# Attention scores and probabilities as pairs of 64-row products, k without masks, PSUM banks divided three, two and three

## The chip, the cores and the metric

One Trainium2 chip, of which the program uses one core. TensorE (PE in the traces, its weight loads PEld) multiplies and transposes; VectorE (DVE), ScalarE (ACT) and GpSimd (POOL) work on tensors; SyncE (SP) issues nearly all DMA. PSUM, where TensorE writes, has eight banks of 128 partitions x 512 float32. The metric is the device time of one execution in microseconds (us), lower is better. The kernel before takes 1148.17 us in the median of three runs (1147.83 to 1148.45).

## The reference

Three layers, one after the other, all in float32:

```
k_p, v_p = mean of k, v over groups of 8 positions            # (4, 8, 72, 64)
attn     = softmax(q @ k_p.T / 8)                             # (4, 8, 576, 72)
x        = (attn @ v_p), heads side by side                   # (2304, 512)

p   = domain_probs / domain_probs.sum(-1)
x   = sum over 4 experts e of  p[:, e] * (relu(x @ w1[e]) @ w2[e])     # 512 -> 1024 -> 512

out = (((x @ g_w1) * (x @ g_w2)) @ g_w3) @ g_wout             # 512 -> 1024 -> 1024 -> 512
```

Four batches, eight heads of 64, 576 positions each; so 2304 tokens of 512 numbers. Pooling leaves 72 keys for each head.

## The kernel before

**Stages.** The tokens are cut into 18 tiles of 128 and six blocks of 384 (three tiles). Attention is done tile by tile. A lead does tiles 0 to 2 alone; the other tiles are slipped into the first expert, whose units (one block, one of eight slices of 128 hidden columns) follow each other in `run_first`: `begin_unit` makes 12 products for a hidden slice, `end_unit`, two units later, 9 products into three accumulators of the block (L1212). Between the steps stands a gap, and `hooks[n]` lists the attention pieces of gap n. The lists are written out in the code (L690 to L726); no planner decides. After the first expert come the other three experts, a stage on w3 and w_out, and the gated layer; none of these is touched, except that their ring of eight PSUM banks (`bank_r`) runs over the banks in another division.

**Attention of one batch.** `load_k` brings the pooled rows in five chunks, four of 128 rows (a row is head and key) and a tail of 64; `pool_k` adds eight positions into one row of 64. Then it makes a row of 128 with the 64 numbers twice, times a mask `mk`: the left copy stays where the head is even, the right where it is odd, zeros elsewhere. Batch 0 does this on VectorE (sum) and GpSimd (mask); batch 1 on GpSimd, with the mask on ScalarE for four chunks (`mask_k`); batches 2 and 3 as batch 0. `make_kT` turns each chunk with a TensorE transpose; column j of kT then has its 64 numbers in partitions 0 to 63 for an even head, 64 to 127 for an odd one.

**Attention of one tile.** q of a tile is laid out as four pairs of heads, the even head's 64 numbers in the lower partitions, the odd one's in the upper. `scores`: one product for each pair, 128 rows deep, 144 columns (72 keys of each head; the zeros of the mask keep the heads apart). Two pairs fill one bank, four heads in a half. Tiles 4 and 13 straddle two batches and do it once for each half of the tokens, on 64 of the 128 output partitions. `exps`: maximum, subtraction and exponential, half by half. `sums`, `normalise`: division by the sum. `attn_T`: eight transposes (one per head, 128 tokens x 72 to 72 x 128), four to a bank, two pieces called one after the other, each followed by a ScalarE eviction into `at_t`. `attend`: for each pair of heads two products of 72 rows into the two halves of the output partitions (x_ps), then a split of the result into a high and a low part.

**PSUM banks.** Eight banks: q0 to q3 by name, and a pool p of four that are handed out in turn. During the first expert the hidden slices use q0 and q1, the attention q2 and q3 in turn (`spare`, cut to two at L1169, in the lead all eight), the three accumulators of a block three of the four in p, one further each time. The second half of batch 1's kT takes one of p.

Of the kernel before, what the change touches and what calls it, by code (L numbers as in the profile page):

```python
# [17 lines left out]
def fused_kernel(  # L18
# [16 lines left out]
    nc = tc.nc  # L35
# [295 lines left out]
    with tc.manual_schedule():  # L331
# [5 lines left out]
            ("at", (H // 2) * BLK * 4, 2), ("e", H * NK * 4, 3), ("kT", NCH * P * 4, 2), ("vp", H * D * 4, 2), ("qT", NP * P * 4, 1),  # L337
            ("kp", D * 4, 4), ("mx", H * 4, 2), ("sm", H * 4, 3), ("hm", NCH * H * 4, 1), ("mk", NCH * 2 * 4, 1),
# [14 lines left out]
        hm = ap.tile([P, NCH, H], F32, tag="hm", name="hm", bufs=1)  # L353
        nc.gpsimd.memset(hm, 1.0)
        nc.gpsimd.affine_select(out=hm, in_=hm, pattern=[[P, NCH], [-NK, H]], compare_op=ALU.is_ge,
                                fill=0.0, base=0, channel_multiplier=1)
        nc.gpsimd.affine_select(out=hm, in_=hm, pattern=[[-P, NCH], [NK, H]], compare_op=ALU.is_ge,
                                fill=0.0, base=NK - 1, channel_multiplier=-1)
        mk = ap.tile([P, NCH, 2], F32, tag="mk", name="mk", bufs=1)
        nc.vector.tensor_reduce(mk, hm.rearrange("p c (a b) -> p c b a", b=2), axis=AX.X, op=ALU.add)  # L360

# [49 lines left out]
        def pool_k(b, c, eng=nc.vector):  # L411
            if c == 0:
                kb_t[b] = ap.tile([P, NCH, 2, D], F32, tag="kb", name="kb", bufs=1)
# [22 lines left out]
        kp_t = {}  # L436

        def mask_k(c):
            for a in range(2):
                nc.scalar.activation(kb_t[1][:, c, a], kp_t[c], AF.Copy, scale=mk[:, c, a:a + 1])  # L440

        def make_kT(b, g0, g1):
            if g0 == 0:
                kT_t[b] = ap.tile([P, NCH * P], F32, tag="kT", name="kT")
            pt = bank_p("kT_ps") if b == 1 and g0 else bank("kT_ps")
# [5 lines left out]
            nc.scalar.activation(kT_t[b][:, g0 * P:g1 * P], pt[:, :(g1 - g0) * P], AF.Copy, scale=LOGIT)  # L451
# [71 lines left out]
        def scores(t):  # L523
            qT = qT_t.pop(t)
            sc_t[t] = []
            for half in range(2):
                sc = bank("sc")
                for hp in range(2 * half, 2 * half + 2):
                    for off, n, b, s in segments(t * P, P):
                        nc.tensor.matmul(sc[off:off + n, (hp % 2) * W:(hp % 2 + 1) * W],  # L530
                                         qT[:, hp, off:off + n], kT_t[b][:, hp * W:(hp + 1) * W],
                                         start=True, stop=True)
                sc_t[t].append(sc)
# [34 lines left out]
        def attn_T(t, half):  # L568
            i, o = divmod(t, TPB)
            if o == 0:  # L570
                at_t[i, half] = ap.tile([P, G, BLK], F32, tag="at", name="at")
# [66 lines left out]
        def do_turn(t):  # L638
            return [(None, lambda half=half: attn_T(t, half)) for half in range(2)]
# [22 lines left out]
        def weight(eng):  # L662
            return [(None, lambda: stream.split(eng))]
# [20 lines left out]
        def lower():  # L684
# [10 lines left out]
                + do_qT(3) + k1[:4] + do_attend(0) + [(None, lambda: rest_of_q.pop(0)())] + weight(VE) + [(None, lambda: mask_k(0)), (None, lambda: rest_of_q.pop(0)())])  # L695
# [4 lines left out]
        hooks[0] = [(None, lambda c=c: mask_k(c)) for c in range(1, NCH - 2)]  # L700
# [12 lines left out]
        hooks[at[TPB + 2] + 3][:0] = [hooks[at[TPB + 2] + 2].pop()]  # L713
# [455 lines left out]
        spare[:] = spare[:2]  # L1169
# [392 lines left out]
```

## Time and profile before

| what | value |
|---|---|
| runs | 1147.83, 1148.17, 1148.45 us |
| the profiled execution | 1147.9 us, its span 1146.1 us |
| TensorE busy | 1139.6 us (99%) |
| VectorE, ScalarE, GpSimd busy | 793.1, 376.0, 416.8 us |
| granted TensorE clock | 1.00 throughout |
| chain that ended last | 96% TensorE |
| score products (L530) | 160, from 10.4 to 160.6 us |
| transposes of probabilities (L575) | 144, from 16.6 to 174.8 us |
| x_ps products (L587) | 128, from 20.7 to 179.4 us |

The span runs from the first to the last instruction; the execution's own time has 1.8 us more around it. TensorE's instructions overlap: the duration in a row includes the way through the array, so the cost of one is read from its start to the start of the next. A row of the timeline that covers several instructions begins with the first and ends with the last; the time from its start to the start of the next row is what the group took. A float32 product appears as two matmuls in the trace, a transpose as one.

### The profile page before, as it was taken

The numbers are of one execution on the slowest core, as the hardware profiler recorded it, in microseconds if no ns is written. First come the engines' busy times: TensorE is split into PE (matmuls) and PEld (weight loads), VectorE is DVE, ScalarE is ACT, GpSimd is POOL, SyncE is SP. The second block draws the span as 40 slices with busy tenths as digits, with TensorE's granted clock in tenths as the row PEclk, the third lists the DMA queues.
The fourth block names the chain that finished last, engine by engine and source line by source line (L and its number), as shares of the span: only waits on it lengthen the run. The fifth ranks groups of instructions, "written<-read, shape, count | busy, mean of one in ns | idle before, by whom it ended". The sixth has DMA issues, their size and how long they took to land.

```text
span 1146.1 us, 17173 instructions
## 1 busy us (share of the span) xinstructions
PE 1139.6 (99%) x5985; PEld 1032.0 (90%) x5985; DVE 793.1 (69%) x1456; ACT 376.0 (33%) x672; POOL 416.8 (36%) x381
## 2 busy tenths in 40 slices
PE   8999999999999999999999999999999999999998
PEld 7898888999899898989898989989889999999997
DVE  7776544867768598658679578877786675774554
ACT  5643432345313053504134421314353313230110
POOL 6765213334525166524336642515001111331211
PEclk9999999999999999999999999999999999999999
DMA  9965515445966726495854578785476165947341
GB/s 229 229 148 123 186 62 197 166 152 183 322 220 196 235 80 181 142 316 167 263 152 123 182 237 192 238 208 146 145 195 230 43 261 209 333 152 288 112 166 56
DMA packets 211555, 213.85 MB, mean 187 GB/s; under 512 B 86596, under 2 KB 166796, under 8 KB 211468
## 3 DMA queue, kind: packets, MB, share of 16 engines
q1 hardware_dynamic: 211180, 212.23, 59.6%
q8 instruction: 47, 0.77, 0.3%
q10 hardware_dynamic: 288, 0.52, 0.1%
q14 instruction: 40, 0.33, 0.1%
HBM read 140.87 MB, written 71.83 MB: 186 GB/s over the span
## 4 chain that ended last, share of the span: by engine, by line
PE 96%; DVE 1%; POOL 1%; ACT 1%; DMA 0%; issue 0%; POOLq 0%
PE g L176 18%; PE g L174 18%; PE g L175 18%; PE s L174 13%; PE s L175 13%; PE s L176 13%; PE sc L530 1%; PE x_ps L587 1%; PE at_ps L575 1%; ACT ap L549 0%; DVE ap L419 0%; DMA stxh<-in_k_dram 0%; DVE ap L543 0%; POOL stxh L422 0%; POOL stxh L421 0%
## 5 line engine op out<-in xcount | busy, mean ns | idle before, releaser
L1014 DVE TENSOR_TENSOR plain<-s,plain 128x384 f32<-128x384 f32 x300 | 158.4, 554 | 83.5 <-PE s L176 35.4
L180 POOL TENSOR_TENSOR round<-x5l,round 128x768 fp32r<-128x768 f32 x60 | 112.2, 1870 | 271.5 <-ACT round L179 254.6
L176 PE MATMUL s<-xo,wl 128*128 128x384 f32 x624 | 208.6, 334 | 0.0
L174 PE MATMUL s<-xo,wh 128*128 128x384 f32 x624 | 208.6, 334 | 0.0
L175 PE MATMUL s<-xo,wh 128*128 128x384 f32 x624 | 208.5, 334 | 0.0
L174 PE MATMUL g<-w2l,round 128*128 128x512 f32 x522 | 204.8, 392 | 0.0
L176 PE MATMUL g<-w2h,round 128*128 128x512 f32 x522 | 203.8, 390 | 0.0
L175 PE MATMUL g<-w2h,round 128*128 128x512 f32 x522 | 203.5, 390 | 0.0
L174 PEld LDWEIGHTS s<-xo,wh 128*128 128x128 f32 x624 | 117.1, 188 | 0.5
L175 PEld LDWEIGHTS s<-xo,wh 128*128 128x128 f32 x624 | 117.1, 188 | 0.5
L176 PEld LDWEIGHTS s<-xo,wl 128*128 128x128 f32 x624 | 117.1, 188 | 0.0
L176 PEld LDWEIGHTS g<-w2h,round 128*128 128x128 f32 x522 | 97.9, 188 | 20.7
L174 PEld LDWEIGHTS g<-w2l,round 128*128 128x128 f32 x522 | 98.0, 188 | 20.0 <-issue 0.8
L175 PEld LDWEIGHTS g<-w2h,round 128*128 128x128 f32 x522 | 98.0, 188 | 19.4
L292 POOL TENSOR_TENSOR x5l<-x5l,x5h 128x256 uint32<-128x256 uint32 x80 | 60.6, 757 | 136.6 <-DVE x5h L291 128.3
L1018 ACT ACTIVATE plain<-s 128x384 f32<-128x384 f32 x60 | 29.2, 487 | 231.4 <-PE s L176 195.5
L179 ACT ACTIVATE round<-x5l 128x768 fp32r<-128x768 f32 x60 | 50.9, 848 | 147.7 <-DVE x5l L1422 146.6
L180 POOL TENSOR_TENSOR round<-plain,round 128x768 fp32r<-128x768 f32 (+1 forms) x29 | 52.5, 1812 | 117.7 <-ACT round L179 101.7
L286 DVE TENSOR_SCALAR x5l<-x5h 128x256 uint32<-128x256 uint32 x80 | 52.9, 662 | 50.3 <-DMA gate<-x5l 28.9
L1014 DVE TENSOR_TENSOR x5l<-s,plain 128x384 f32<-128x384 f32 x120 | 65.6, 556 | 24.8 <-PE s L176 18.3
L1260 ACT ACTIVATE plain<-plain 128x768 f32<-128x768 f32 x36 | 30.5, 848 | 111.3 <-DVE plain L1014 111.3
L174 PE MATMUL g<-xl,round 128*128 128x384 f32 x192 | 66.1, 344 | 0.0
(257 smaller groups left out, 2211.8 us busy)
## 6 DMA issues: line engine op xcount, KB each, us to landing
xo<-keptx SPq DMA_DIRECT2D x42, 768.0 KB
raw<-in_moe_w_dram SPq DMA_DIRECT2D x54, 256.0 KB
keptx<-xo SPq DMA_DIRECT2D x12, 768.0 KB
x5h<-in_moe_w_dram SPq DMA_DIRECT2D x128, 64.0 KB
x5h<-in_moe_w_dram SPq DMA_DIRECT2D x32, 256.0 KB
ob<-acc SPq DMA_DIRECT2D x24, 256.0 KB
kept<-xo SPq DMA_DIRECT2D x8, 768.0 KB
xo<-kept SPq DMA_DIRECT2D x8, 768.0 KB
```

The source lines that it names most:

```text
L174: nc.tensor.matmul(ps, lh, rl, start=first, stop=False)
L175: nc.tensor.matmul(ps, lh, rh, start=False, stop=False)
L176: nc.tensor.matmul(ps, ll, rh, start=False, stop=last)
L179: nc.scalar.activation(hi, src, AF.Copy)
L180: (lo_eng or nc.vector).tensor_tensor(lo, src, hi.bitcast(F32), op=ALU.subtract)
L286: nc.vector.tensor_scalar(au, h, 0x7FFFFFFF, None, op0=ALU.bitwise_and)
L292: nc.gpsimd.tensor_tensor(au, au, l, op=ALU.add)
L530: nc.tensor.matmul(sc[off:off + n, (hp % 2) * W:(hp % 2 + 1) * W], qT[:, hp, off:off + n], kT_t[b][:, hp * W:(hp + 1) * W], start=True, st ...
L575: nc.tensor.transpose(pt[:NK, g * P:(g + 1) * P], e[:, half * G + g, :], ident)
L1014: nc.vector.tensor_tensor(to, one, two, op=ALU.add)
L1018: nc.scalar.activation(x, product(j, A11, B11), AF.Copy)
L1260: nc.scalar.activation(r, r, AF.Relu)
```

## The change

- **k.** `pool_k` sums in three additions (256, 128, 64 columns), the last of which writes the row of 64 twice, with no mask. `mk`, `hm`, `kp`, `mask_k` and GpSimd's mask products are gone. The tail of 64 rows is transposed as 64 rows, and its columns alone are copied.
- **Scores.** For each pair of heads two products of 64 rows and 72 columns, the even head on partitions 0 to 63 into one bank, the odd head on 64 to 127 into another. A bank holds the four even or the four odd heads of all pairs, so the order of heads in `e` becomes even heads, then odd.
- **Probabilities.** Each of the eight transposes becomes two, of tokens 0 to 63 and 64 to 127, in two banks that alternate; one piece instead of two; the evictions write eight heads of 64 tokens each. `at_t` is one tile for a block.
- **Banks.** q0 to q4 and a pool p of three. The attention has q2, q3, q4 in turn during the first expert, the accumulators always the same three.

TensorE's rows at the end of the lead before (qT_ps turns q, sc are scores, vp_ps sums v, at_ps turns probabilities, x_ps is attention times v):

```order
L530 MATMUL sc<-ap_72,plain 128x144 x4
L509 MATMUL qT_ps<-ident,stxh 128x128 x4
L530 MATMUL sc<-ap_72,plain 128x144 x8
L469 MATMUL vp_ps<-stxl,ident 72x192 x8
L575 MATMUL at_ps<-ident,ap_72 72x128 x8
L469 MATMUL vp_ps<-stxl,ident 72x64 x8
L575 MATMUL at_ps<-ident,ap_72 72x128 x16
L587 MATMUL x_ps<-ap_72 64x384 x8
```

The same place now:

```order
L505 MATMUL sc<-ap_72,plain 128x72 x8
L485 MATMUL qT_ps<-ident,stxh 128x128 x4
L505 MATMUL sc<-ap_72,plain 128x72 x16
L445 MATMUL vp_ps<-stxl,ident 72x192 x8
L552 MATMUL at_ps<-ident,ap_72 72x64 x16
L445 MATMUL vp_ps<-stxl,ident 72x64 x8
L552 MATMUL at_ps<-ident,ap_72 72x64 x32
L564 MATMUL x_ps<-ap_72 64x384 x8
```

Nothing changes places; scores and transposes become twice as many and half as wide.

VectorE's first rows, where k of batch 0 is summed for the lead (stxh, stxl are the landing places), before:

```order
L360 TENSOR_REDUCE ap_72<-ap_72 128x10
L419 TENSOR_REDUCE ap_72<-stxh 128x64 x3
L419 TENSOR_REDUCE ap_72<-stxl 128x64
L419 TENSOR_REDUCE ap_72<-stxl 64x64
L512 COPY plain<-qT_ps 128x512
```

And now (the same three for each of the chunks between):

```order
L406 TENSOR_TENSOR stxl<-stxl 128x256
L406 TENSOR_TENSOR stxl<-stxl 128x128
L408 TENSOR_TENSOR plain<-stxl 128x128
L406 TENSOR_TENSOR stxl<-stxl 64x256
L406 TENSOR_TENSOR stxl<-stxl 64x128
L408 TENSOR_TENSOR plain<-stxl 64x128
L488 COPY plain<-qT_ps 128x512
```

Five reductions become fifteen additions, and VectorE itself writes what GpSimd wrote (plain).

TensorE early in the first expert, transposes of tile 4 and scores of tile 6 (g are the expert's accumulators and hidden slices), before:

```order
L176 MATMUL g_682<-xh,round 128x384
L575 MATMUL at_ps<-ident,ap_72 72x128 x4
L174 MATMUL g_524<-w2l,round 128x512
L175 MATMUL g_524<-w2h,round 128x512
L176 MATMUL g_524<-w2h,round 128x512
```

```order
L176 MATMUL g_526<-w2h,round 128x512
L575 MATMUL at_ps<-ident,ap_72 72x128 x4
L530 MATMUL sc<-ap_72 128x144 x4
L174 MATMUL g_747<-xl,round 128x384
L175 MATMUL g_747<-xh,round 128x384
```

And now:

```order
L176 MATMUL g_736<-xh,round 128x384
L552 MATMUL at_ps<-ident,ap_72 72x64 x16
L174 MATMUL g_558<-w2l,round 128x512
L175 MATMUL g_558<-w2h,round 128x512
L176 MATMUL g_558<-w2h,round 128x512
```

```order
L176 MATMUL g_560<-w2h,round 128x512
L505 MATMUL sc<-ap_72 128x72 x8
L174 MATMUL g_813<-xl,round 128x384
L175 MATMUL g_813<-xh,round 128x384
```

The second half of the transposes no longer stands nine accumulating products behind the first.

The diff, cut to its core:

```diff
-    ps_p = ctx.enter_context(tc.tile_pool(name="ps_p", bufs=KC, space=PSUM))
+    ps_p = ctx.enter_context(tc.tile_pool(name="ps_p", bufs=TPB, space=PSUM))
...
-        return bank_p(name) if m < 4 else bank_q(m - 4, name)
+        return bank_p(name) if m < TPB else bank_q(m - TPB, name)
...
-        spare = [lambda n, m=m: bank_q(m, n) for m in (2, 3, 0, 1)] + [bank_p] * KC
+        spare = [lambda n, m=m: bank_q(m, n) for m in (2, 3, 4, 0, 1)] + [bank_p] * TPB
...
-            kp = ap.tile([P, D], F32, tag="kp", name="kp")
-            if n < P and b == 0:
-                nc.gpsimd.memset(kb_t[b][n:, c], 0.0)
-            if eng is nc.vector:
-                eng.tensor_reduce(kp[:n], r[:n, :].rearrange("p (r d) -> p d r", d=D), axis=AX.X, op=ALU.add)
-            else:
-                eng.tensor_tensor(r[:n, :256], r[:n, :256], r[:n, 256:], op=ALU.add)
-                eng.tensor_tensor(r[:n, :128], r[:n, :128], r[:n, 128:256], op=ALU.add)
-                eng.tensor_tensor(kp[:n], r[:n, :64], r[:n, 64:128], op=ALU.add)
-            if b == 1 and c < NCH - 2:
-                kp_t[c] = kp
-                return
-            (eng if b == 1 else nc.gpsimd).tensor_tensor(kb_t[b][:n, c], kp[:n].unsqueeze(1).broadcast_to([n, 2, D]),
-                                    mk[:n, c].unsqueeze(2).broadcast_to([n, 2, D]), op=ALU.mult)
+            kb = kb_t[b][:n, c]
+            for m in (256, 128):
+                eng.tensor_tensor(r[:n, :m], r[:n, :m], r[:n, m:2 * m], op=ALU.add)
+            one, two = (r[:n, m:m + D].unsqueeze(1).broadcast_to([n, 2, D]) for m in (0, D))
+            eng.tensor_tensor(kb, one, two, op=ALU.add)
...
-        def mask_k(c):
-            for a in range(2):
-                nc.scalar.activation(kb_t[1][:, c, a], kp_t[c], AF.Copy, scale=mk[:, c, a:a + 1])
...
-                nc.tensor.transpose(pt[:, (c - g0) * P:(c - g0 + 1) * P],
-                                    kb_t[b][:, c].rearrange("p a d -> p (a d)"), ident)
+                n = min(P, NROW - c * P)
+                nc.tensor.transpose(pt[:, (c - g0) * P:(c - g0) * P + n],
+                                    kb_t[b][:n, c].rearrange("p a d -> p (a d)"), ident[:n, :n])
...
-            for half in range(2):
-                sc = bank("sc")
-                for hp in range(2 * half, 2 * half + 2):
-                    for off, n, b, s in segments(t * P, P):
-                        nc.tensor.matmul(sc[off:off + n, (hp % 2) * W:(hp % 2 + 1) * W],
-                                         qT[:, hp, off:off + n], kT_t[b][:, hp * W:(hp + 1) * W],
+            sc_t[t] = [bank("sc") for _ in range(2)]
+            for hp in range(NP):
+                for off, n, b, s in segments(t * P, P):
+                    for a, sc in enumerate(sc_t[t]):
+                        nc.tensor.matmul(sc[off:off + n, hp * NK:(hp + 1) * NK], qT[a * D:(a + 1) * D, hp, off:off + n],
+                                         kT_t[b][a * D:(a + 1) * D, (2 * hp + a) * NK:(2 * hp + a + 1) * NK],
                                          start=True, stop=True)
...
-        def attn_T(t, half):
+        def attn_T(t):
...
-            pt = bank("at_ps")
-            for g in range(G):
-                nc.tensor.transpose(pt[:NK, g * P:(g + 1) * P], e[:, half * G + g, :], ident)
-            src = pt[:NK].rearrange("p (g s) -> p g s", s=P)
-            dst = at_t[i, half][:NK, :, o * P:(o + 1) * P]
-            nc.scalar.activation(dst, src, AF.Copy)
+            pts = [bank("at_ps") for _ in range(2)]
+            R = P // 2
+            for g in range(H):
+                for n, pt in enumerate(pts):
+                    rows = slice(n * R, (n + 1) * R)
+                    nc.tensor.transpose(pt[:NK, g * R:(g + 1) * R], e[rows, g, :], ident[rows, rows])
+            for n, pt in enumerate(pts):
+                at = o * P + n * R
+                nc.scalar.activation(at_t[i][:NK, :, at:at + R], pt[:NK].rearrange("p (g s) -> p g s", s=R), AF.Copy)
...
-                                     at_t[i, hp // 2][:NK, 2 * (hp % 2) + a, off:off + n], start=True, stop=True)
+                                     at_t[i][:NK, a * G + hp, off:off + n], start=True, stop=True)
...
-        hooks[at[TPB + 2] + 3][:0] = [hooks[at[TPB + 2] + 2].pop()]
...
-        spare[:] = spare[:2]
+        spare[:] = spare[:3]
```

## Rows read from the trace of the kernel before

**Rows 1.** The page: the chain that ended last, by engine.

```profile
PE 96%; DVE 1%; POOL 1%; ACT 1%; DMA 0%; issue 0%; POOLq 0%
```

**Rows 2.** Timeline of TensorE, plain blocks: start us, us, engine, line, operation, count.

```profile
100.52 1.14 PE L530 MATMUL sc<-ap 128*128 128x144 f32 x8
101.40 0.43 PE L174 MATMUL g<-xl,round 128*128 128x384 f32 x1
101.67 0.34 PE L175 MATMUL g<-xh,round 128*128 128x384 f32 x1
101.84 0.34 PE L176 MATMUL g<-xh,round 128*128 128x384 f32 x1
...
127.43 1.03 PE L575 MATMUL at_ps<-ident,ap 128*72 128x128 f32 x8
128.22 0.42 PE L174 MATMUL g<-xl,round 128*128 128x384 f32 x1
128.48 0.33 PE L175 MATMUL g<-xh,round 128*128 128x384 f32 x1
```

**Rows 3.** Timeline of TensorE, x_ps and the scores of tile 13.

```profile
119.11 0.39 PE L176 MATMUL g<-w2h,round 128*128 128x512 f32 x1
119.43 2.80 PE L587 MATMUL x_ps<-ap 72*64 72x384 f32 x16
122.06 1.15 PE L530 MATMUL sc<-ap 128*64 128x144 f32 x16
123.14 0.50 PE L174 MATMUL g<-w2l,round 128*128 128x512 f32 x1
123.47 0.39 PE L175 MATMUL g<-w2h,round 128*128 128x512 f32 x1
123.70 0.40 PE L176 MATMUL g<-w2h,round 128*128 128x512 f32 x1
```

**Rows 4.** Timeline of TensorE, the end of the lead; in brackets idle and releaser.

```profile
17.44 1.20 PE L469 MATMUL vp_ps<-stxl,ident 72*72 72x64 f32 x16
18.47 1.92 PE L575 MATMUL at_ps<-ident,ap 128*72 128x128 f32 x16
20.72 0.54 PE L587 MATMUL x_ps<-ap 72*64 72x384 f32 x2 [0.33 <-ACT ap L578]
```

**Rows 5.** Timeline of TensorE's weight loads behind tile 13.

```profile
123.14 0.19 PEld L174 LDWEIGHTS g<-w2l,round 128*128 128x128 f32 x1 [0.20 <-issue]
123.25 0.19 PEld L175 LDWEIGHTS g<-w2h,round 128*128 128x128 f32 x1
```

**Rows 6.** Timeline of TensorE, three places where it stands still.

```profile
39.31 0.60 PE L575 MATMUL at_ps<-ident,ap 128*72 128x128 f32 x4
40.09 0.63 PE L575 MATMUL at_ps<-ident,ap 128*72 128x128 f32 x4 [0.18 <-ACT ap L549]
...
42.47 0.34 PE L176 MATMUL g<-xh,round 128*128 128x384 f32 x1
42.82 1.22 PE L530 MATMUL sc<-ap 128*128 128x144 f32 x8
...
50.99 0.66 PE L530 MATMUL sc<-ap 128*128 128x144 f32 x4
51.83 0.76 PE L530 MATMUL sc<-ap 128*128 128x144 f32 x4 [0.19 <-ACT ap L578]
```

**Rows 7.** Timeline of ScalarE and TensorE between two blocks.

```profile
207.34 2.06 ACT L753 ACTIVATE plain<-g,plain 128x512 f32<-128x512 f32 x3 [1.63 <-DVE xo L910]
...
211.09 0.39 PE L174 MATMUL g<-w2l,round 128*128 128x512 f32 x1
```

**Rows 8.** Timeline of VectorE and GpSimd, k in the lead, an addition at 30.20.

```profile
7.25 1.94 DVE L419 TENSOR_REDUCE ap<-stxl 128x64 f32<-128x512 f32 x2
...
9.27 0.39 POOL L427 TENSOR_TENSOR plain<-ap 64x128 f32<-64x128 f32 x1 [0.27 <-DVE ap L419]
...
11.21 0.95 DVE L543 TENSOR_REDUCE ap<-sc 128x4 f32<-128x288 f32 x2 [0.91 <-PE sc L530]
...
30.20 0.28 DVE L427 TENSOR_TENSOR plain<-ap 64x128 f32<-64x128 f32 x1
```

**Rows 9.** Timeline of ScalarE, evictions at the end of the lead.

```profile
19.11 2.05 ACT L578 ACTIVATE ap<-at_ps 72x512 f32<-72x512 f32 x4 [0.20 <-PE at_ps L575]
```

More of the change, by code (lines that the diff above doesn't have):

```diff
@@ L336, in fused_kernel @@
         ap = Places(**packed(ap1, [
-            ("at", (H // 2) * BLK * 4, 2), ("e", H * NK * 4, 3), ("kT", NCH * P * 4, 2), ("vp", H * D * 4, 2), ("qT", NP * P * 4, 1),
-            ("kp", D * 4, 4), ("mx", H * 4, 2), ("sm", H * 4, 3), ("hm", NCH * H * 4, 1), ("mk", NCH * 2 * 4, 1),
+            ("at", H * BLK * 4, 1), ("e", H * NK * 4, 3), ("kT", NCH * P * 4, 2), ("vp", H * D * 4, 2), ("qT", NP * P * 4, 1),
+            ("mx", H * 4, 2), ("sm", H * 4, 3),
             ("sp", NTILE * 4, 1), ("side", 2 * P * 4, 1)], 4 * XO),
@@ L350, in bank @@
             return spare[(turn[0] - 1) % len(spare)](name)
[L353 to L360, printed above, removed]
         staging = [home.tile([P, 3, 512], F32, tag=f"x{i}{t}", name="stx" + t) for i in (NB - 1, NB - 2, NB - 3) for t in "hl"]
@@ L412, in pool_k @@
             if c == 0:
-                kb_t[b] = ap.tile([P, NCH, 2, D], F32, tag="kb", name="kb", bufs=1)
+                kb_t[b] = ap.tile([P, NCH, 2, D], F32, tag="kb", name="kb")
             r, n = in_t.pop(("k", b, c))
-            kp = ap.tile([P, D], F32, tag="kp", name="kp")
-            if n < P and b == 0:
-                nc.gpsimd.memset(kb_t[b][n:, c], 0.0)
-            if eng is nc.vector:
-                eng.tensor_reduce(kp[:n], r[:n, :].rearrange("p (r d) -> p d r", d=D), axis=AX.X, op=ALU.add)
-            else:
-                eng.tensor_tensor(r[:n, :256], r[:n, :256], r[:n, 256:], op=ALU.add)
-                eng.tensor_tensor(r[:n, :128], r[:n, :128], r[:n, 128:256], op=ALU.add)
-                eng.tensor_tensor(kp[:n], r[:n, :64], r[:n, 64:128], op=ALU.add)
-            if b == 1 and c < NCH - 2:
-                kp_t[c] = kp
-                return
-            (eng if b == 1 else nc.gpsimd).tensor_tensor(kb_t[b][:n, c], kp[:n].unsqueeze(1).broadcast_to([n, 2, D]),
-                                    mk[:n, c].unsqueeze(2).broadcast_to([n, 2, D]), op=ALU.mult)
+            kb = kb_t[b][:n, c]
[3 more added lines that the diff above has]
+            eng.tensor_tensor(kb, one, two, op=ALU.add)
         warm_ps = []
@@ L434, in turn_ident @@
                 nc.tensor.transpose(pw[:, :P], ident, ident)
-        kp_t = {}
-        def mask_k(c):
-            for a in range(2):
-                nc.scalar.activation(kb_t[1][:, c, a], kp_t[c], AF.Copy, scale=mk[:, c, a:a + 1])
         def make_kT(b, g0, g1):
@@ L444, in make_kT @@
                 kT_t[b] = ap.tile([P, NCH * P], F32, tag="kT", name="kT")
-            pt = bank_p("kT_ps") if b == 1 and g0 else bank("kT_ps")
+            pt = bank("kT_ps")
             for c in range(g0, g1):
-                nc.tensor.transpose(pt[:, (c - g0) * P:(c - g0 + 1) * P],
-                                    kb_t[b][:, c].rearrange("p a d -> p (a d)"), ident)
+                n = min(P, NROW - c * P)
+                nc.tensor.transpose(pt[:, (c - g0) * P:(c - g0) * P + n],
+                                    kb_t[b][:n, c].rearrange("p a d -> p (a d)"), ident[:n, :n])
                 if b == 0 and c < NCH - 2:
                     turn_ident(warm_ps[0], 3)
-            nc.scalar.activation(kT_t[b][:, g0 * P:g1 * P], pt[:, :(g1 - g0) * P], AF.Copy, scale=LOGIT)
+            end = min(g1 * P, NROW)
+            nc.scalar.activation(kT_t[b][:, g0 * P:end], pt[:, :end - g0 * P], AF.Copy, scale=LOGIT)
         def pool_v(b, h, eng):
@@ L566, in normalise @@
                 eng.tensor_tensor(e_t[t][:, some], e_t[t][:, some], sm_t[t][:, some].unsqueeze(2).broadcast_to([P, h[1] - h[0], NK]), op=ALU.mult)
-        def attn_T(t, half):
+        def attn_T(t):
             i, o = divmod(t, TPB)
             if o == 0:
-                at_t[i, half] = ap.tile([P, G, BLK], F32, tag="at", name="at")
+                at_t[i] = ap.tile([P, H, BLK], F32, tag="at", name="at")
             e = e_t[t]
-            pt = bank("at_ps")
-            for g in range(G):
-                nc.tensor.transpose(pt[:NK, g * P:(g + 1) * P], e[:, half * G + g, :], ident)
-            src = pt[:NK].rearrange("p (g s) -> p g s", s=P)
-            dst = at_t[i, half][:NK, :, o * P:(o + 1) * P]
-            nc.scalar.activation(dst, src, AF.Copy)
+            pts = [bank("at_ps") for _ in range(2)]
[7 more added lines that the diff above has]
+                nc.scalar.activation(at_t[i][:NK, :, at:at + R], pt[:NK].rearrange("p (g s) -> p g s", s=R), AF.Copy)
         def attend(i, hp):
@@ L638, in do_turn @@
         def do_turn(t):
-            return [(None, lambda half=half: attn_T(t, half)) for half in range(2)]
+            return [(None, lambda: attn_T(t))]
         def do_attend(i):
@@ L694, in fused_kernel @@
                 + do_turn(1) + do_turn(2)
-                + do_qT(3) + k1[:4] + do_attend(0) + [(None, lambda: rest_of_q.pop(0)())] + weight(VE) + [(None, lambda: mask_k(0)), (None, lambda: rest_of_q.pop(0)())])
+                + do_qT(3) + k1[:4] + do_attend(0) + [(None, lambda: rest_of_q.pop(0)())] + weight(VE) + [(None, lambda: rest_of_q.pop(0)())])
         V1 = 5
@@ L699, in fused_kernel @@
         hooks[1] = k1[4:] + do_qT(TPB + 1)
-        hooks[0] = [(None, lambda c=c: mask_k(c)) for c in range(1, NCH - 2)]
         at = {TPB: 0, TPB + 1: 5, TPB + 2: 8}
```

2 lines of the change are left out of this document (removed).

## The prediction

> **What bounds the kernel now.** I read the chain of waits first [rows 1]: TensorE is 96% of it, and every other engine has 1% or less. So a change counts where it lengthens or shortens TensorE's own stream, or where TensorE stands still. All attention lies in the first 180 us: a lead in which TensorE works on attention alone and waits for others, until the products x_ps of block 0 start at 20.72 behind an idle 0.33 [rows 4], and then blocks whose attention products are slipped between the expert's own. After that the program is the same in both kernels. Next I read TensorE's timeline, start to start, since the durations in it overlap [rows 2, 3].
>
> **Price of a plain block.** Eight score products of 144 columns start at 100.52, the next expert product at 101.40, and the one behind it 0.27 later where 0.17 is normal (101.67 to 101.84): 0.88 + 0.10 = 0.98 us, 0.1225 each [rows 2]. (The trace shows each float32 product of the program as two, each transpose as one.) Eight transposes cost 0.79 (127.43 to 128.22) and 0.26 instead of 0.17 behind them: 0.88, 0.11 each [rows 2]. Going in and out costs nothing here.
>
> **Price of a side-by-side block.** No product in before uses half of the rows; x_ps uses half of the columns, so do the scores of two tiles. These do run in pairs: 16 products of 384 columns take 119.43 to 122.06, 2.63 us, or 0.16 each, where 0.1225 for 144 columns would make 0.33 [rows 3]. But entering and leaving is not free. The product before x_ps is followed after 0.32 instead of 0.23 (123.47 to 123.70): 0.09. The pairs should take 8 x 0.327 = 2.61, so 0.02 to 0.05 more. The 16 score products of tile 13, in the same half-column arrangement, take 1.08 where 8 x 0.1225 is 0.98: 0.10 at the way out; and the next product is late by 0.10 (0.33 against 0.23). Together 0.34 us for one way in and out [rows 3].
>
> **The change, steady blocks (tiles 3 to 17).**
> Scores: 16 products of 72 columns in 8 pairs. The columns alone would need 0.061 a pair. But each still loads 128 weight columns, and two loads of 128 columns started 0.11 apart where nothing else held them (123.14, 123.25) [rows 5]. A load for 64 rows does not occur in before. Bounds of a pair: 0.061, if half the rows load in half the time; 0.22, if the two loads stand in a queue. I take 0.11, the nearest row, loads of both halves at once as the half-column pairs do. 8 x 0.11 + 0.34 = 1.22 against 0.98: +0.24. For the 13 tiles inside one batch: +3.1 us.
> The Trainium skill, "TensorE: Matmul & The Clock Gate", section LDWEIGHTS, says that a load's time goes by its columns, not by the rows of the contraction. By that rule a 64-row load keeps the full time and the sum stands; were it by cells, the first rival below would be the sum. The trace agrees with the rule's time for 128 columns (128 columns at 1.2 GHz, an estimate by that page of 0.107 us; 0.11 seen) and shows nothing of 64 rows.
> Tiles 4 and 13 straddle two batches and become 64 x 64 products, four at once, with loads of 64 columns: 8 x 0.061 + 0.34 = 0.83 against 0.98 + 0.34 = 1.32 for tile 4: -0.49. Tile 13 now shares the arrangement of the x_ps ahead of it, pays no way in, and afterwards pays about half a switch: 0.49 + 0.17 = 0.66 against 0.98: -0.3. Bounds: 0 if only two run at once.
> Probabilities: 16 transposes of 64 columns in 8 pairs, weights of 72 columns. Nearest row: 16 products with 72 weight columns and 64 moving columns, 17.44 to 18.47, 0.064 each [rows 4]; half of 0.11 is 0.055. I take 0.06: 8 x 0.06 + 0.34 = 0.82 against 0.88: -0.06, x 15 = -0.9. Bounds: 0.12 a pair without overlap, and 0.5 without any switch cost.
> k's last chunk is now a 64-row transpose behind four plain ones: one switch more, 0.34 - 0.05, x 3 = +0.9.
> In three blocks scores follow x_ps directly; the way out of x_ps (0.20) and the way into the scores become one switch: -0.2 x 3 = -0.6.
> Together 3.1 - 0.5 - 0.3 - 0.9 + 0.9 - 0.6 = +1.7.
>
> **Banks.** Early on TensorE waits where the ring of two banks comes round: transposes at 40.09 for the exponentials that still read a score bank (0.78 for four, 0.34 too much), scores at 51.83 for an eviction (0.84 for four, 0.35 too much) [rows 6]. With three banks, alternating from the first product, the bank in question was released two users earlier, and the mask products leave ScalarE in just that stretch. Both waits go: -0.7. Next in line there is TensorE itself. Bounds: 0 to -1.0, with the smaller wait at 42.82 [rows 6].
> Three fixed accumulators instead of four in turn: block i+1 then needs the bank that block i just filled. The three evictions start at 207.34 and take 2.06, the first about 0.7, so it is free at 208.0; the next block's first product is at 211.09 [rows 7]. The expert's two hidden products lie between, so it costs 0; without that cover, 0.7 in each of five blocks.
> The mask products of GpSimd and ScalarE beyond the lead: off the chain [rows 1], 0.
>
> **The lead.** Its end is one for one the start of TensorE's unbroken stream.
> - GpSimd's mask step goes. The last sum on VectorE ends at 9.19, the mask product runs at 9.27 for 0.39 [rows 8]; a direct handover saves about 0.45.
> - VectorE sums k by three additions for one reduction at 0.95 (two in 1.94) [rows 8]. The row for an addition of 128 columns has 0.28 [rows 8]; for 256 columns between 0.28 and 0.55, I take 0.4. 0.96 for 0.95: 0. Bounds for five chunks: -1.0 (0.2 less each) to +0.8.
> - The scores of tile 0 no longer finish half by half. Now the first half is ready at 11.21 [rows 8], after four products of eight; then only after all: a switch in (0.2) and four more pairs, +0.5. VectorE and ScalarE have a backlog from there on, so all shifts.
> - The probabilities of tile 2 too come as two banks that finish together. Now four evictions run 19.11 to 21.16 and x_ps starts at 20.72, after the third [rows 4, 9]. Then every x_ps product needs heads from both banks, so all four, and the first starts about 0.25 later: 21.45, +0.75.
> Sum: -0.45 + 0 + 0.5 + 0.75 = +0.8.
>
> **Sum.** +1.7 - 0.7 + 0.8 = +1.8 us. The profiled execution took 1147.9 us (span 1146.1 and 1.8 around): 1149.7. The median of the runs is 0.3 above it, within their spread of 0.6.
>
> **Rivals.**
> 1. Half-row loads are hidden, columns set the pace. For: a block of rows half as high holds half the weights; against: rows 5. Scores 8 x 0.061 + 0.34 = 0.83, -0.15 x 13 = -2.0 instead of +3.1, lead 0.3 better: 1149.7 - 5.4 = 1144.3.
> 2. A switch by rows costs half of one by columns (0.17). For: rows are split, outputs keep all their partitions; against: what is seen at the way in and out looks like the array running empty and a load standing open [rows 3, 5], which any rearrangement would need. 0.17 less in 28 blocks, 0.5 in kT, 0.3 in tiles 4 and 13 and the lead together, 0.3 given back behind x_ps: -5.3, 1144.4. With rival 1 as well: 1139.
> 3. Slower: the two halves don't run side by side, so the change doesn't do what it says. It decides from the point where a pair costs more than 0.13 for scores. For: only column pairs are seen; against: those overlap fully [rows 3]. Scores 16 x 0.11 + 0.34 = 2.1, +1.12 x 13 = 14.6; probabilities 16 x 0.06 + 0.34 = 1.3, +0.42 x 15 = 6.3; tiles 4 and 13 +0.2; kT, x_ps and banks -0.4; lead +2.2: +22.9, 1171.
> The Trainium skill, "TensorE: Matmul & The Clock Gate", "Packing small matmuls", reports row tiles that run concurrently, loads too when the row group differs. By that rule rival 3 falls; no run here shows it.
>
> **How the numbers follow.** A time 0.2% off, 2.3 us, is about what can be told from no change here: 1145.9 to 1150.5 counts as the same. Forecast 0.45, with its own range of 1147 to 1152.5 (0.26 same, 0.17 slower, 0.02 faster). Rival 1: 0.18 (0.13 faster, 0.05 same). Rival 2: 0.14 (0.10, 0.04). Both: 0.07 faster. Rival 3: 0.10 slower. The rest, 0.06, is a lead far better or worse than priced: 0.03 faster, 0.01 same, 0.02 slower. Faster 0.35, same 0.36, slower 0.29. The range 1140 to 1156 leaves out rival 3 and the lower half of both together.
>
> **What would show it.** In TensorE's timeline after: scores start to start at 0.11 a pair, the two of a pair almost together; 0.061 says rival 1, 0.22 rival 3. The product behind a block late by 0.2 in all, the one ahead by 0.1; half of that says rival 2. Transposes at 0.06 a pair. x_ps of block 0 near 21.5. No stall at the places of rows 6; a stall of the first accumulating product of a block would break the cover I named. If TensorE's stretch from x_ps to the end of block 5 grows by more than 4 us or shrinks, the block prices are wrong.

## The result, and the profile after

The changed kernel takes 1154.89 us in the median of four runs (1152.85 to 1155.52), the kernel before 1148.04 beside it: a ratio of 1.0056, 95% interval 1.0039 to 1.0074. It is 6.9 us slower. The wide range of 1140 to 1156 held the time. The forecast of 1149.7 was 5.2 too low, and the forecast's own range of 1147 to 1152.5 missed it.

Where the 6.9 us arise is read by following the expert products, which are the same and in the same order in both traces: the start of each product after, less the start of the same product before.

| place | before | after | behind by |
|---|---|---|---|
| first product x_ps of block 0 | 20.72 | 21.72 | 1.00 |
| eighth expert product of the program | 24.78 | 29.03 | 4.25 |
| first expert product behind the last transposes | 174.84 | 179.88 | 5.04 |
| first product of the stage after the first expert | 269.13 | 274.44 | 5.31 |
| two products of the gated stage | 916.47, 962.00 | 922.15, 968.83 | 5.68, 6.83 |

So 1.0 us is lost in the lead, 3.3 within the eight microseconds behind it, 0.8 in all the attention blocks together (150 us), and 1.8 where the two programs are the same. The chain of waits of the changed kernel:

```profile
PE 93%; DVE 3%; DMA 2%; ACT 1%; SPq 1%; issue 0%; POOL 0%; DVEq 0%; ACTq 0%
```

TensorE had 96% of it before, and DMA 0% [rows 1]: the chain now crosses a load late in the program.

**The blocks.** TensorE's timeline after, a block of scores and one of transposes, to be held against [rows 2]:

```profile
54.17 0.39 PE L176 MATMUL g<-w2h,round 128*128 128x512 f32 x1
54.49 1.12 PE L505 MATMUL sc<-ap 64*128 64x72 f32 x16
55.54 0.45 PE L174 MATMUL g<-xl,round 128*128 128x384 f32 x1
55.82 0.34 PE L175 MATMUL g<-xh,round 128*128 128x384 f32 x1
...
132.01 0.34 PE L176 MATMUL g<-xh,round 128*128 128x384 f32 x1
132.28 0.64 PE L552 MATMUL at_ps<-ident,ap 64*72 64x64 f32 x16
132.85 0.45 PE L174 MATMUL g<-xl,round 128*128 128x384 f32 x1
133.13 0.34 PE L175 MATMUL g<-xh,round 128*128 128x384 f32 x1
```

Scores: the way in 0.32 for 0.23, so 0.09; the block 1.05; behind it 0.28 for 0.17, so 0.11. Together 1.25 us, where 1.22 was forecast and 0.98 stood. Start to start, the two products of a pair are 0.007 apart and the pairs 0.112 (the first step, 0.167, left aside). Transposes: 0.10, 0.57 and 0.11, together 0.78 where 0.82 was forecast and 0.88 stood. Tile 13 behind x_ps, whose place before is [rows 3]:

```profile
124.50 2.80 PE L564 MATMUL x_ps<-ap 72*64 72x384 f32 x16
127.23 0.73 PE L505 MATMUL sc<-ap 64*64 64x72 f32 x32
127.90 0.50 PE L174 MATMUL g<-w2l,round 128*128 128x512 f32 x1
```

32 products in 0.67: the 64 x 64 products start four at a time, 0.007 apart, and the groups follow each other every 0.063 (the first after 0.114).

**The lead.** The same view, where x_ps of block 0 begins; the place of [rows 4]:

```profile
18.70 0.64 PE L552 MATMUL at_ps<-ident,ap 64*72 64x64 f32 x16
19.60 0.95 PE L552 MATMUL at_ps<-ident,ap 64*72 64x64 f32 x16 [0.26 <-DVE ap L540]
21.72 5.00 PE L564 MATMUL x_ps<-ap 72*64 72x384 f32 x16 [1.17 <-ACT ap L555]
26.65 0.69 PE L174 MATMUL g<-xl,round 128*128 128x384 f32 x1
...
28.74 0.46 PE L174 MATMUL g<-xl,round 128*128 128x384 f32 x1
29.03 0.34 PE L175 MATMUL g<-xh,round 128*128 128x384 f32 x1
```

x_ps starts 1.0 late, behind an idle 1.17, and then its 16 products take 4.93 (21.72 to 26.65) where before took 2.73 (20.72 to 23.45). The expert products behind it come every 0.32 instead of 0.17 until 28.74. The busy times by stretch show the granted clock beside it. Columns: stretch, its length, busy time and count of TensorE, its loads, VectorE, ScalarE and GpSimd, then the granted clock, DMA share and GB/s.

```profile
20.30:21.70 1.40, 0.25 (x8) 0.10 (x4) 0.95 (x1) 1.23 (x3) 1.24 (x3) 1.00 0.92 328
21.70:26.60 4.90, 4.88 (x16) 1.59 (x16) 1.67 (x3) 1.48 (x3) 4.59 (x9) 0.55 1.04 299
26.60:28.70 2.10, 2.10 (x8) 2.05 (x7) 1.21 (x2) 1.01 (x2) 1.94 (x4) 0.50 0.27 50
28.70:40.00 11.30, 11.30 (x99) 9.98 (x99) 8.67 (x15) 7.51 (x27) 4.39 (x7) 0.99 0.69 198
```

TensorE stood nearly still (0.25 of 1.40 us busy) before 21.7; then its clock was at half, 1.2 GHz for 2.4, for most of 7 us (0.55 and 0.50). In the kernel before, the clock was 1.00 there.

**A new stall and a late load.** TensorE's timeline at the transposes near 110:

```profile
109.71 0.25 PE L552 MATMUL at_ps<-ident,ap 64*72 64x64 f32 x1
110.49 0.61 PE L552 MATMUL at_ps<-ident,ap 64*72 64x64 f32 x15 [0.53 <-DVE ap L525]
```

VectorE's, just before:

```profile
105.92 1.42 DVE L406 TENSOR_TENSOR stxl<-stxl 128x256 f32<-128x256 f32 x2
107.38 0.36 DVE L408 TENSOR_TENSOR plain<-stxl 128x128 f32<-128x128 f32 x1
...
109.88 0.46 DVE L525 TENSOR_TENSOR ap<-sc,ap 128x288 f32<-128x288 f32 x1
```

ScalarE's late in the gated stage, and the product of TensorE's that comes late behind it:

```profile
959.46 0.53 ACT L937 ACTIVATE round<-x5h 128x384 fp32r<-128x384 f32 x1 [5.27 <-DMA x5h<-turned]
961.37 0.85 ACT L938 ACTIVATE round<-x5h 128x768 fp32r<-128x768 f32 x1 [1.38 <-DMA x5h<-turned]
...
968.83 0.44 PE L174 MATMUL s<-z,wh 128*128 128x384 f32 x1 [0.87 <-DVE z L180]
```

The three additions for k of one chunk take 1.42 (two of them) and 0.36, where a chunk takes 0.99 in the lead (6.50 to 7.49). VectorE comes late to the scores, and the second transpose comes 0.74 late, behind the subtraction (L525) that reads the bank it needs. At the end, ScalarE waits for a load 1.38 (before: 0.53), and TensorE's product at 968.83 comes 1.21 behind the one ahead of it.

### The profile page after: what moved, and what is told of

Same layout as the page of the kernel before. It is cut to its first block, busy times and chain, and to the rows that moved or that the text cites. A ratio compares the mean times of both kernels' runs of the same rounds, so it can differ in the third digit from the quotient of the medians.

```text
span 1153.1 us, 17783 instructions
## 1 busy us (share of the span) xinstructions
PE 1144.1 (99%) x6289; PEld 1025.1 (89%) x6289; DVE 797.7 (69%) x1486; ACT 374.9 (33%) x666; POOL 411.0 (36%) x361
## 4 chain that ended last, share of the span: by engine, by line
PE 93%; DVE 3%; DMA 2%; ACT 1%; SPq 1%; issue 0%; POOL 0%; DVEq 0%; ACTq 0%
PE g L174 18%; PE g L176 17%; PE g L175 17%; PE s L174 13%; PE s L176 13%; PE s L175 13%; PE x_ps L564 2%; PE sc L505 1%; DMA x5h<-turned 1%; PE at_ps L552 1%; DMA raw<-in_moe_w_dram 1%; SPq L454 0%; DMA stxl<-in_v_dram 0%; DVE stxl L406 0%; DVE z L180 0%
## 5 line engine op out<-in xcount | busy, mean ns | idle before, releaser
L286 DVE TENSOR_SCALAR x5l<-x5h 128x256 uint32<-128x256 uint32 x80 | 48.8, 610 | 49.0 <-DMA gate<-x5l 27.4
```

What stands on the lines that cost most here:

```text
L286: nc.vector.tensor_scalar(au, h, 0x7FFFFFFF, None, op0=ALU.bitwise_and)
```

## The experiments

The kernel before took 1148.2 to 1148.4 us in the medians beside them, and ratios are to it. All but the ones that say "before" start from the changed kernel.

### Work in place of the wait ahead of x_ps

```diff
+        def fill():
+            turn_ident(bank("fill"), 9)
...
-                + do_turn(1) + do_turn(2)
+                + do_turn(1) + do_turn(2) + [(None, fill)]
```

Nine transposes of the identity, read by nothing, stand where TensorE waited.

> The changed kernel with nine transposes of the identity into a spare bank between the transposes of tile 2 and the first x_ps product. In the changed kernel TensorE stands idle there for 1.2 us, and from about 22 us to 28.7 us its granted clock is half. Theory W (the wait lowers the clock): with the wait filled the granted clock stays at 1.00 in 21.7 to 28.7, all x_ps pairs of block 0 start 0.32 apart, the first expert product starts near 24.5 instead of 26.65, and the time is 3.3 us below the changed kernel's 1154.9: 1151.6. Theory P (the half-row products lower it, full rows or not in between): the clock falls all the same, 1154 to 1155.

Measured 1151.42 (1151.06 to 1152.28), ratio 1.0027 [1.0017, 1.0037]: 3.5 less. The timeline of TensorE in this kernel:

```profile
20.37 1.20 PE L414 MATMUL fill<-ident 128*128 128x128 f32 x9
21.61 2.80 PE L564 MATMUL x_ps<-ap 72*64 72x384 f32 x16
24.34 0.44 PE L174 MATMUL g<-xl,round 128*128 128x384 f32 x1
```

Its stretches, in the columns above:

```profile
20.30:21.70 1.40, 1.37 (x17) 1.06 (x13) 1.14 (x1) 1.12 (x3) 1.24 (x3) 1.00 0.89 304
21.70:26.60 4.90, 4.90 (x28) 3.02 (x28) 2.89 (x5) 2.49 (x5) 4.60 (x7) 1.00 1.00 295
```

x_ps starts hardly earlier (21.61) and takes 2.73 again. The transposes of the lead are still in pairs, so they alone don't lower the clock. The later start of x_ps cost 1.0; standing still ahead of it cost 3.3 more (the eighth expert product is 4.25 behind the kernel before without the filler, 0.90 with it).

### Whole transposes in the lead

```diff
+            if t < LEAD:
+                return [(None, lambda half=half: attn_T_plain(t, half)) for half in range(2)]
             return [(None, lambda: attn_T(t))]
```

attn_T_plain is the transpose of before, eight of 128 tokens, four to a bank, evicted into the new at_t.

> The changed kernel with the transposes of tiles 0 to 2 as before (eight of 128 tokens, half by half), the other tiles in pairs. By my reading of the lead the four evictions no longer have to end before x_ps starts: x_ps at 20.9 instead of 21.7. Theory W: so the wait is as short as before (0.3 us), the clock stays at 1.00, and the time is 0.8 + 3.3 us below the changed kernel: 1150.8. Theory P with the score pairs as cause: the clock is half all the same, 1154.

Measured 1152.25 (1151.46 to 1152.89), 1.0032 [1.0019, 1.0045]. The clock is 1.00 throughout and x_ps starts at 21.24 behind an idle 0.30, which bears out the cause:

```profile
21.24 2.96 PE L574 MATMUL x_ps<-ap 72*64 72x384 f32 x15 [0.30 <-ACT ap L550]
```

But it is 1.4 us slower than expected, and the 0.8 that a shorter lead was to give back did not come. In the order of heads of the change each half of the transposes holds one head of every pair, so x_ps needs all four evictions here too: its first product starts after the third, but the next at 21.73, just behind the end of the fourth (21.68). The first expert product comes at 24.45, no earlier than with the filler (24.34). Scores at 43.75 then wait 0.70 for a bank that ScalarE still reads, which they don't in the changed kernel. A product at 920.7 in the gated stage comes 1.37 behind the one ahead of it; against the changed kernel that is made up for, since the late product at 968.83 is on time here.

### The banks alone, in the kernel before

```diff
-    ps_p = ctx.enter_context(tc.tile_pool(name="ps_p", bufs=KC, space=PSUM))
+    ps_p = ctx.enter_context(tc.tile_pool(name="ps_p", bufs=TPB, space=PSUM))
...
-        spare[:] = spare[:2]
+        spare[:] = spare[:3]
```

> The kernel before with the banks alone: five named banks and a pool of three, attention on three banks, accumulators fixed. My sum: the waits at 40.1, 42.8 and 51.8 us go, 0.7 to 1.0 us; the fixed accumulators cost nothing: 1147.1 where before is 1148.04. Rival F (the fixed accumulators wait for their evictions): 0.7 us in each of five blocks against the gain, 1150.5. Rival N: the stalls only move, 1148.0.

Measured 1148.09 (1147.73 to 1148.91), 0.9997 [0.9988, 1.0006]: nothing gained. Its timeline, at the places of [rows 6] and two others:

```profile
33.26 0.40 PE L176 MATMUL g<-w2h,round 128*128 128x512 f32 x1
34.29 1.20 PE L530 MATMUL sc<-ap 128*64 128x144 f32 x16 [0.63 <-ACT ap L451]
...
39.69 1.03 PE L575 MATMUL at_ps<-ident,ap 128*72 128x128 f32 x8
40.48 0.42 PE L174 MATMUL g<-xl,round 128*128 128x384 f32 x1
...
51.10 1.15 PE L530 MATMUL sc<-ap 128*128 128x144 f32 x8
51.98 0.43 PE L174 MATMUL g<-xl,round 128*128 128x384 f32 x1
...
268.55 0.39 PE L176 MATMUL g<-w2h,round 128*128 128x512 f32 x1
269.07 0.44 PE L174 MATMUL s<-xo,wh 128*128 128x384 f32 x1
```

Both stalls that I named are gone, 0.38 and 0.45 us. In their place the scores at 34.29 wait for an eviction of kT, which puts TensorE 0.30 later behind them, and the first product of the next stage comes 0.52 behind the last one (before 0.23), another 0.29. The stall moved. The second place belongs to the banks: the gap there is 0.37 to 0.68 in every profile with the new division, and 0.23 in the two without it.

### The paired transposes alone, in the kernel before

```diff
-            return [(None, lambda half=half: attn_T(t, half)) for half in range(2)]
+            return [(None, lambda: attn_T(t))]
```

attn_T is that of the change, with its one tile at_t, and the hook that moved half of tile 4's transposes goes; scores, k, banks and the order of heads are those of before.

> The kernel before with the transposes of the probabilities in pairs of 64 tokens alone (scores, masks, banks as before). From the changed kernel's trace a block of them costs 0.78 us against 0.88: 15 x -0.10 = -1.5 us in the steady part. In the lead x_ps waits for all four evictions, +0.75. Theory W: TensorE waits there for over 1 us and the clock falls, another +3.3: 1150.6. Theory P (score pairs lower the clock): no fall, 1147.3. With only two banks for the attention a pair needs both at once, so a wait of up to 0.4 us in some tiles may come on top.

Measured 1149.21 (1146.28 to 1151.09), 1.0009 [1.0000, 1.0017]. The start of x_ps, and the stretches:

```profile
21.69 3.41 PE L590 MATMUL x_ps<-ap 72*64 72x384 f32 x16 [1.16 <-ACT ap L581]
...
20.30:21.70 1.40, 0.24 (x10) 0.08 (x6) 0.99 (x1) 1.20 (x3) 1.24 (x3) 1.00 0.89 330
21.70:26.60 4.90, 4.90 (x21) 2.64 (x22) 2.69 (x6) 2.90 (x7) 4.59 (x9) 0.71 1.01 303
26.60:28.70 2.10, 2.10 (x14) 2.10 (x13) 0.30 (x1) 0.36 (x2) 1.94 (x4) 0.87 0.66 145
```

The clock falls without any score pair, behind the same wait (1.16); so it is the transposes' late evictions, not the scores. It came back sooner here, and over the eleven runs the mean granted clock goes from 1.000 (1146.28 us) to 0.995 and 0.996 (1148.9 to 1151.1): the spread of the times goes with the clock.

### All scores as 64 x 64 products, four at once

```diff
-                for off, n, b, s in segments(t * P, P):
+                for off, n, b in [(o + m, D, b) for o, n, b, s in segments(t * P, P) for m in range(0, n, D)]:
```

> The changed kernel with every tile's scores cut at 64 tokens as well: 64 x 64 products, four at once, as the change makes them for the tiles that straddle two batches. Moving columns stay 72, weight columns fall from 128 to 64. Theory L (a pair of half-row score products is held up by its weight loads, by their columns): each group comes every 0.065 us instead of 0.112, a block costs 0.86 instead of 1.25, 13 x -0.39 = -5.1 us against the changed kernel's 1154.9, the low clock in the lead left as it is: 1149.8. Rival O (the 0.112 is a fixed cost of a half-row pair, whatever it loads): twice the products in the same rhythm, 16 x 0.056 or more, so no gain or a loss: 1155 and above.

Measured 1150.03 (1147.56 to 1152.27), 1.0016 [1.0007, 1.0025]: 4.9 less. Part of this comparison is the clock, whose mean goes from 0.996 (1151.9 to 1152.3 us) to 1.000 (1147.6 and 1148.0) over these eleven runs; free of it, the two kernels with the filler and the reduction (below) differ by 4.8 for the same edit. The score block:

```profile
101.24 0.40 PE L176 MATMUL g<-w2h,round 128*128 128x512 f32 x1
101.56 0.73 PE L505 MATMUL sc<-ap 64*64 64x72 f32 x32
102.22 0.44 PE L174 MATMUL g<-xl,round 128*128 128x384 f32 x1
102.50 0.34 PE L175 MATMUL g<-xh,round 128*128 128x384 f32 x1
```

The block takes 0.66 for 1.05, with the same ways in and out. The products are twice as many, the columns that stream through each quarter of the array the same; only the columns of a load are halved. So the load of 128 columns set the pace of the pairs, and half the rows made it no cheaper. With 64 columns the groups come every 0.063, which is about what their 72 moving columns need (0.061 by the prediction's price), so this pace no longer measures the load.

The profile of this kernel holds two long waits of TensorE. Behind that of 1.17 us ahead of x_ps (21.28) the clock falls to 0.62 and 0.50, as in the changed kernel. Behind one of 1.18 us between expert products (108.02, again for the subtraction) it stays at 1.00.

### Whole transposes everywhere

```diff
-            return [(None, lambda: attn_T(t))]
+            return [(None, lambda half=half: attn_T_plain(t, half)) for half in range(2)]
```

> The changed kernel with the probabilities of all tiles transposed as before (128 tokens, half by half), scores still in pairs. If the wait before x_ps alone lowers the clock, it stays at 1.00 here, 1150.8 from the lead (1154.9 - 3.3 - 0.8), and the 15 steady blocks of transposes give back their 0.10 each: 1152.3. If the score pairs lower the clock: 1155.

Measured 1151.96 (1151.69 to 1152.88), 1.0032 [1.0020, 1.0045], with the clock at 1.00. The pairs of scores lower no clock. The forecast came out by luck: the 0.8 of the lead did not come back here either (first expert product at 24.35), and the late product of 968.83, on time here, made up for it. Score pairs, new k, order of heads and banks together lose 3.6 us; by the block price the score pairs alone are worth 13 x 0.27 = 3.5 of that, an estimate.

### Banks and paired transposes from tile 3, in the kernel before

```diff
+            if t < LEAD:
+                return [(None, lambda half=half: attn_T_plain(t, half)) for half in range(2)]
+            return [(None, lambda: attn_T(t))]
```

With the bank lines above; scores and k as before.

> The kernel before with the banks of the change, and transposes in pairs from tile 3 on, plain in the lead; masks and scores as before. Block prices of the changed kernel: 15 x -0.10 = -1.5; banks 0 as measured; lead and clock as before: 1146.7 where before is 1148.3. If a switch costs more than it looked where it stands next to plain scores: 1148 and above.

Measured 1146.94 (1146.52 to 1148.12), 0.9987 [0.9978, 0.9995]: 1.4 less than before, with the clock at 1.00. The half of the change that pays is the transposes, once the lead is left alone. The profile, of the slowest of these runs, holds a wait that is longer than the one ahead of x_ps in the changed kernel, and the clock does not fall behind it:

```profile
35.61 1.17 PE L530 MATMUL sc<-ap 128*64 128x144 f32 x15 [1.33 <-ACT round L179]
...
28.70:40.00 11.30, 9.97 (x64) 8.85 (x64) 8.16 (x17) 7.63 (x33) 7.04 (x10) 1.00 0.96 234
```

It stands behind expert products that follow each other without a gap, the other at the end of the lead. So the length of a wait alone does not decide; what does was not tried.

### Filler, and k of batches 2 and 3 by one reduction

```diff
+            if b > 1:
+                kp = ap.tile([P, D], F32, tag="kp", name="kp")
+                eng.tensor_reduce(kp[:n], r[:n, :].rearrange("p (r d) -> p d r", d=D), axis=AX.X, op=ALU.add)
+                nc.gpsimd.tensor_copy(kb, kp[:n].unsqueeze(1).broadcast_to([n, 2, D]))
+                return
```

> The changed kernel with the lead's wait filled by nine identity transposes (1151.4 by itself), and k of batches 2 and 3 summed by one VectorE reduction, then written twice by GpSimd without mask, instead of three VectorE additions. Theory D (the additions hold up VectorE: 1.42 + 0.36 us a chunk beside GpSimd against 1.05, and so the subtraction that frees a score bank at 110 us): TensorE's stall of 0.6 us at 110 us goes, 1150.8. Rival: the stall is the ring of three banks itself and stays, 1151.4.

Measured 1150.95 (1150.25 to 1151.92), 1.0021 [1.0012, 1.0029]: 0.5 less than with the filler alone, though the intervals of the two overlap. In the profile the stall is gone from TensorE's timeline, and the expert product behind it gains 0.74 on the kernel with the filler alone:

```profile
107.23 0.64 PE L557 MATMUL at_ps<-ident,ap 64*72 64x64 f32 x16
107.80 0.50 PE L174 MATMUL g<-w2l,round 128*128 128x512 f32 x1
```

### The changed kernel once more

> The changed kernel once more, unaltered, for a second profile on the same chip as the two others. Theory (the clock falls because TensorE stands still before x_ps of block 0): the granted clock is again about half from 21.7 to 28.7 us, and the time 1154.9 within 0.5. Rival (the fall was a chance of one run): 1.00 there and 1151.5. The wait of 0.9 us late in the gated stage, which the first profile showed, either recurs at the same product, and belongs to the program, or moves, and is chance.

Measured 1155.43 in the median of six (1151.26 to 1155.89), 1.0052 [1.0040, 1.0064]. The stretches of its profile:

```profile
20.30:21.70 1.40, 0.24 (x4) 0.21 (x4) 0.68 (x1) 1.07 (x2) 1.24 (x4) 0.71 0.95 313
21.70:26.60 4.90, 4.90 (x16) 1.51 (x14) 1.55 (x3) 1.47 (x3) 4.59 (x8) 0.50 1.04 284
26.60:28.70 2.10, 2.10 (x8) 1.89 (x7) 1.34 (x3) 1.01 (x2) 1.94 (x4) 0.50 0.22 35
```

The clock fell again. One run of the six shows a mean granted clock of 1.000 and took 1151.26; the other five, at 0.996 and 0.997, took 1154.11 to 1155.89. So the same program is some 4 us faster when the clock happens to hold, and the fall is likely but not certain. The late wait of the gated stage did not recur: the product that came 1.21 late follows after 0.20 here, and a wait of 0.57 stands at 291.90 instead, for ScalarE. How late the product is belongs to the run, but where it can be late is fixed: the two products of the table above each stand behind a load. The first of them follows after 0.17 or 0.18 in six of the profiles, the kernel before among them, and after 0.26 (this run), 0.37, 0.43, 0.44 (the first profile of the change), 0.58, 1.26 and 1.37 in the others, all of them kernels that start from the change. Why is open.

### Both repairs and the four-way scores

Two kernels with the 64 x 64 scores and the reduction for batches 2 and 3: one with whole transposes in the lead, one with the filler.

> The changed kernel with three edits together: scores as four 64 x 64 products, plain transposes in the lead (two banks filled one after the other), and k of batches 2 and 3 summed by one reduction with a copy on GpSimd. Theory (loads go by columns; the wait in the lead lowers the clock; additions beside GpSimd are slow): the three effects are at different places and add up. From the changed kernel's 1154.9: quads -4.9, clock and lead -2.7, reduction -0.5 gives 1146.8, about 1.4 below the kernel before. Rival (the quads only hide what the clock did, since block 0's products run at half clock in both): 1148 or more. Rival (quads also shorten the wait of the lead): 1146.

> As the one before, but with nine filler transposes ahead of x_ps in place of the plain transposes of the lead. From the kernel with filler and reduction, 1150.95, less 4.9 for the quads: 1146.1. If the late waits that the kernel with plain transposes in the lead showed (1.2 us at the gated stage) go with its lead, this one is faster than the other by 0.5 to 1; if they come and go from run to run, the two are within 0.5.

Whole transposes: 1147.11 (1145.89 to 1148.04), 0.9990 [0.9981, 0.9999]. Filler: 1146.17 (1145.88 to 1147.26), 0.9982 [0.9973, 0.9991], 2.0 us below the kernel before and the fastest here. The three effects add up: 3.5, 4.9 and 0.5 from 1154.9 give 1146.0. The first one is 0.9 slower in the median, but the intervals overlap. In its profile a product at 913.7 in the gated stage comes 1.26 behind the one ahead of it, as in the other kernel with that lead; yet this is its fastest run (1145.89), so the wait does not account for the median. The profile of the second holds a wait of 1.07 us at 33.08, for GpSimd's sums of batch 1, with the clock at 1.00 behind it.

## Why the prediction was right or wrong

**Luck in the number.** The wide range reached up to 1156, but no term of the sum and no named rival gives 1154.9; the forecast's own range stopped at 1152.5. What the prediction had priced came near: 1.0 in the lead, 0.8 in the blocks and 0.24 at the change of stage are +2.0 for +1.8. The 3.3 of the clock and the late waits were not in it. Its own sign, a stretch from x_ps to the end of block 5 longer by more than 4 us, came up (4.07) and would have blamed the block prices; 3.25 of it is the clock.

**Block prices: right.** Scores +0.27 a block for +0.24, the pace 0.112 for the 0.11 that I took, what is left for the ways in and out 0.35 (1.25 less 8 x 0.112) for 0.34. Rivals 1, 2 and 3 are refuted by these rows: loads are not hidden, the switch is not half, and the pairs run side by side. The Trainium skill, "TensorE: Matmul & The Clock Gate", section LDWEIGHTS, had said that a load goes by its columns; the traces agree: 64 rows with 128 columns keep 0.112 a pair, and with 64 columns a group of four comes every 0.063. Transposes gained 0.10 a block for 0.06. kT cost +0.29 each as forecast (0.73 and 0.11 behind it). Tile 4 gained 0.87 for 0.49: its block of before came to 1.74 with its ways in and out (1.53 of it from 33.50 to 35.03), not to the 1.32 that I reckoned. The arrangement is not dearer than I priced it; tile 13's takes 1.08. The first three matmuls of tile 4 started 0.17 and 0.24 apart while ScalarE was evicting kT (33.32 to 34.13), a wait that I had not seen in before.

**The blocks together: right, from terms that were not.** +0.8 for +1.0. The stalls of [rows 6] went, as forecast. But "VectorE sums k by three additions" was priced for the lead only, and nothing at all for batch 2: there it cost a stall of 0.74, which is gone with one reduction in their place (0.5 in the medians).

**Banks: half right.** The two stalls went (0.83), the gain did not come: with the banks alone 0.60 turned up at two other places, one of them the stage behind the first expert, which my cover of two hidden products does not reach. Of "-0.7", 0 was left in that kernel; that it costs 0 in the later blocks held. In the changed kernel the wait for kT did not appear (tile 4's scores start 0.32 behind the product ahead of them), only the 0.24 at the change of stage.

**The lead: the step that failed.** "All four, and the first starts about 0.25 later: 21.45, +0.75" was right in its mechanism: four evictions, x_ps at 21.72 behind an idle 1.17. The sum, +1.0 for +0.8, is nearer than its terms: the direct handover was to save 0.45, but the scores of tile 0 begin only 0.08 earlier (10.36 for 10.44), since VectorE's additions end at 9.52 where its reductions ended at 9.19. What I left out is the clock of TensorE. The wait was counted as its own length. Standing still there cost 3.3 us more, the largest single term of the result. The filler removes it, and the second measurement of the changed kernel shows the same program with and without it. I had the granted clock in the table of before as 1.00 throughout and never asked what could lower it.

**The end: not foreseen.** 1.8 us where both programs are the same: 0.24 at the change of stage, which the banks explain, and up to 1.5 in late waits that move from run to run. I had cost the rest of the program at nothing, since no line of it is touched; in before ScalarE waited 0.53 for that load, and TensorE's product behind it came after the usual 0.17. That the margin there is small, and a different run of DMA eats it, is my guess; why the changed kernel meets it more often is not settled.

## What to carry to other kernels

A new wait on TensorE is looked at twice: for its length, and for the granted clock behind it. The clock need not fall (waits of 1.07 to 1.33 us within the first expert left it at 1.00), but where it did, here at the end of the lead, it cost another 3.3 us, nearly three times the wait itself. Where other engines need that time anyway, give TensorE something to do and look at the clock again. When small products are to run side by side, first ask what paces them: with half the rows and all the columns of weights the load keeps its time, and only fewer columns make it shorter. A stall that one bank division removes is looked for in the next user of the ring before it is counted as gained.

## What the runs showed of the hardware

- 1.16 or 1.17 us with TensorE idle at the end of the lead, behind short transposes and shorter waits, was followed by up to 7 us at half the granted clock in all four profiles that hold it; by the mean clock the same program kept it at 1.00 in one run of ten. Waits of 0.30 to 0.33 at the same place, and nine transposes in place of the wait, left it at 1.00.
- Waits of 1.33 us (35.61, banks and transposes from tile 3), 1.18 (108.02, four-way scores) and 1.07 (33.08, four-way scores with filler and reduction) within the first expert left the clock at 1.00.
- Four 64 x 64 products of 72 columns run at once, groups every 0.063 us, loads of all four included; two 64 x 128 ones every 0.112.
- An addition of 256 columns and one of 128 on VectorE took 0.74 in the lead and 1.42 at 106 us, the same instructions; GpSimd was busy with additions of its own at the later place. That GpSimd is the cause was not tried by itself.
